# Result stores moved between DMA queues and transfers spaced differently in an attention plus MLP-mixer kernel

## The chip, the cores and the metric

The kernel runs on one core of one Trainium2 chip. The metric is device time in microseconds (us) from start to end of one execution; the median of several runs is given.

The core's engines are named as the profile names them: PE (TensorE, matrix products; PEld is its weight load), DVE (VectorE), ACT (ScalarE), POOL (GpSimd) and SP (SyncE, which only issues transfers here). Each works through its own instruction list in order. SP and ACT also issue DMAs ("SPq" and "ACTq" in the profile); an instruction that waits holds up everything behind it in its engine's list.

## The reference

Attention with normalized queries and keys over 8 batches, 12 heads, 448 positions and head size 64, and then a mixer MLP on the result, all in float32:

```python
q_n, k_n = rmsnorm(q, g_q), rmsnorm(k, g_k)
attn = softmax(q_n @ k_n.T / sqrt(64))
x = (attn @ v), heads side by side          # per batch: 448 x 768
h = relu(x.T @ w_tok1) @ w_tok2             # token mixing: 448 -> 256 -> 448
u = x + h.T
out = u + relu(u @ w_ch1) @ w_ch2           # channel mixing: 768 -> 1536 -> 768
```

## The kernel before, in words

The work goes batch by batch. Attention handles two pairs of heads at a time in four steps; while the mixer of batch b runs, the attention of batch b+1 is interleaved with it. What each engine does, and in which order, is written out by hand: the code builds lists of items, each a function with a cost in microseconds; `merge` interleaves lists so that each advances in proportion to its share of cost, and `run` calls the items in order and adds their costs to a model clock. A function given to `later(us, fn)` is called when that clock has advanced by `us`. The costs serve the interleaving alone.

The activations stand transposed: `uT` holds 768 channels (6 blocks of 128) by 448 positions. For one batch the mixer goes through these stages:

- **x.** The token mixing needs x with positions on the partitions. For batches after the first, DVE transposes 32x32 blocks of `uT` into `xt` (L615), four DMAs write it to memory (`send_x`, L585, tile `xs`, runs of 128 bytes), and one DMA reads it back (`load_x`, L590, 672 KB). This is done in two halves of three blocks, both in the last part of the batch before.
- **Token mixing.** `tok1` (L629, relu by ACT at L632), then six products `tok2` (L637), each added into `uT` by DVE (L642); `moving_sums` (L658 to L661) prepares sums for the next stage. Products use two PSUM banks in turn (`m_ps`), so a product waits until DVE or ACT has emptied the bank of the product two before it.
- **Channel products.** Batches after the first use a seven-product scheme on 2x2 blocks: `ch1` (L761), `ch2` with two column blocks (L818), and last `ch2` with one column block, seven items of 2.24 us that `last_items` lists. The weights come from memory in units of 384 KB (L687); six buffers, and the load of a unit is issued five units ahead.
- **Result.** DVE transposes each of the six blocks of `uT` into a tile `turned` (`trans_y`, L855, four buffers), and four DMAs each (`send_y`, L577, 56 KB, runs of 128 bytes) write it to the output. For all batches but the last, all six are done inside the token mixing of the next batch, and ACT issues their DMAs.

In batch 0 the weights are also split into blocks and stored (L193), and sums of weight blocks are formed by POOL (load L203, sums L206 to L209, store L211); most of these sums fall into batch 1.

Queries and keys are loaded by SP (L1071, for most pairs eight DMAs of 56 KB), each followed by a squares pass on ACT (L1090), row sums on DVE (L1104), a fold on ACT (L1112), a chain of small DVE operations for the inverse root (L1121 to L1147), scaling (L299) and two transposes (L314). Values come by L287. The row sums of the exponentials (L376) are formed by POOL and DVE.

Every DMA of the compiled program signals its landing on one of eight semaphores, given out in turn over both queues, and waits first for the DMA that used its semaphore before.

Of the kernel before, what the change touches and what calls it, by code (L numbers as in the profile page):

```python
# [8 lines left out]
F32 = mybir.dt.float32  # L9
# [35 lines left out]
def whole(ctx, tc, shifted, pre, q, k, v, g_q, g_k, moe_w_tok1, moe_w_tok2, moe_w_ch1, moe_w_ch2, out):  # L45


    nc = tc.nc
# [7 lines left out]
    P = 128  # L56
# [58 lines left out]

    def later(us, fn):

        pending.append((clock[0] + us, fn))

    def run(items):  # L120
        for c, fn in items:
# [341 lines left out]
    def att_step(g):  # L463


        t, s = divmod(g, 4)
        p = 2 * t
        pair = (p, p + 1)
        live = g < NG
        items = []  # L470

        def finish():
            if s == 0 and t:
                last = (p - 2, p - 1)
                for k in (NK - 2, NK - 1):
                    values(last, k)
            if live:
                for k in ((0,), (1, 2), (3, 4), (5, 6))[s]:
                    score(t, k)
            if s == 0 and t:  # L480
                if not on_pe(p - 1):
                    row_sums(t - 1)
                for i in last:
                    st.pop(("v", i))

        def tiled():
            if shifted:
                if live:
                    both_shifted()
            else:  # L490
                finish()
            if live and s == 3:
                for i in pair:
                    st.pop(("qkT", i))
            if inside:
                for fn in turns:
                    fn()
            if live and s and not shifted:
                for k in ((), (0,), (1, 2), (3, 4))[s]:
                    values(pair, k)  # L500

        def both_shifted():
            i = p + s // 2
            if s % 2 == 0:
                score_shifted(i)
                return
            for k in range(NK):
                values((i,), k)
            for k in range((NK + 1) // 2):
                st.pop(("e1", i, k))  # L510
            st.pop(("v", i))
            for part in denominators((i,)):
                part()

        n = p + 2
        ahead, behind, turns = [], [], []
        f = lambda fn, *pairs: [lambda i=i: fn(i, st) for i in pairs]
        scales = lambda n: [lambda i=i: scale(i) for i in (n, n + 1)]  # L520
        if g in (1, 5):
            ahead, behind = f(pre.square, g // 4 * 2 + 4), f(pre.reduce, g // 4 * 2 + 4)
        elif g in (2, 6):
            ahead, behind = f(pre.square, g // 4 * 2 + 5), f(pre.reduce, g // 4 * 2 + 5)
        elif g in (3, 7):
            behind = pre.roots(g // 4 * 2 + 4, st)
        elif g in (4, 8):
            behind = scales(g // 4 * 2 + 2)
        if live and n < NP:
            late = n < 2 * NPAIR + 2  # L530
            if t >= NPAIR // 2 and late:
                if s == 1:
                    ahead, behind = f(pre.square, n), f(pre.reduce, n) + f(pre.square, n + 1)
                elif s == 2:
                    behind = f(pre.reduce, n + 1) + pre.roots(n, st) + scales(n)
            elif t >= NPAIR // 2:
                a, b = f(pre.square, n) + f(pre.reduce, n), f(pre.square, n + 1) + f(pre.reduce, n + 1)
                behind = (a, b + pre.roots(n, st), scales(n), [])[s]
            now = {2: [] if pre.plain(n) else [n], 3: [n, n + 1] if pre.plain(n) else [n + 1]}.get(s, [])
            turns = [lambda q=q, i=i: turn_qk(q, i) for q in now for i in (1, 0)]  # L540

        inside = g < 2 * NPAIR
        items += [(0.3, fn) for fn in ahead]
        items.append((2.4 if s == 1 else 3.2, tiled))
        part = lambda fns, c=0.4: [(c, fn) for fn in fns]
        if s == 0 and t and not shifted:
            items += part(denominators((p - 2, p - 1)))
        if live and not on_pe(p):
            items += [(0.5, lambda k=k: group_sums(t, k)) for k in ((), (1, 2), (3, 4), (5, 6))[s]]

        if s == 0 and 5 < p + 1 < NP:
            items.append((0.0, lambda: load_v(p + 1)))
        if live and s == 1 and 5 < p + 2 < NP:
            items.append((0.0, lambda: load_v(p + 2)))
        js = []
        if live and s == 0:
            js = [n, n + 1] if pre.plain(p) else [n + 1]
        elif live and s == 3 and not pre.plain(n):
            js = [n + 2]
        items += [it for j in js if pre.first_slot + 2 <= j < NP  # L560
                  for it in part(pre.loads(j, st, nc.sync, nc.sync), 0.2)]
        if g == 3:
            items += [it for j in (6, 7) for it in part(pre.loads(j, st, nc.sync, nc.sync), 0.2)]
        items += part(behind)
        if not inside:
            items += part(turns)
        return items
# [4 lines left out]


    def send_y(b, cc, t):
        dst = out[b][:, cc * P:(cc + 1) * P]
        for i in range(0, P, 32):
            nc.scalar.dma_start(  # L577
                out=dst[:, i:i + 32].rearrange("(n t) c -> t n c", t=32),
                in_=t[i:i + 32].rearrange("t (n c) -> t n c", c=32))

    def send_x(b, half, t):

        xs = st["xs"] = xs_pool.tile([KC * S, P], F32, name="xs")
        for i in range(0, P, 32):
            nc.sync.dma_start(  # L585
                out=xs[:, i:i + 32].rearrange("(n t) c -> t n c", t=32),
                in_=t[i:i + 32].rearrange("t (n c) -> t n c", c=32))

    def load_x(b, half):
        nc.sync.dma_start(  # L590
# [7 lines left out]
    def trans_x(b, j):  # L598

        half, o = divmod(j, KC)  # L600
        if b == 0:

            if o == 0:
                x_tile(b, half)
            ps = s_tile("t_ps")
            for c in range(NS):
                nc.tensor.transpose(
                    ps[0:R, c * P:(c + 1) * P], st["uT", b][:, j, c * R:(c + 1) * R], ident[:, :])
            nc.scalar.copy(  # L609
                out=st["x", b, half][0:R, o], in_=ps[0:R, :].rearrange("p (c n) -> p c n", c=NS))  # L610
            return

        if j == 0:
            st["xt"] = tu_pool.tile([P, 2, KC, S], F32, name="xt", tag="tu")
        nc.vector.transpose(out=st["xt"][:, half, o, :], in_=st["uT", b][:, j, :])  # L615
        if o == KC - 1:
            t = st["xt"][:, half].rearrange("p j s -> p (j s)")
            if half:
                st.pop("xt")
            later(2.0, lambda: send_x(b, half, t))  # L620
            later(6.0, lambda: load_x(b, half))

    def tok1(b, jc, h):
        cs = slice(h * HC, (h + 1) * HC)
# [225 lines left out]
            into(nc.vector, 1, 0, got)  # L850

    def trans_y(b, cc):

        t = turn_pool.tile([P, S], F32, name="turned")
        nc.vector.transpose(out=t[:], in_=st["uT", b][:, cc, :])  # L855
        later(2.0, lambda: send_y(b, cc, t))

    def turns(b, cs):
        return [(0.3, lambda cc=cc: trans_y(b, cc)) for cc in cs]

    us = lambda n, cols: n * cols * 4 / 2400

# [21 lines left out]
    def in_next(b):  # L884


        return b < B - 1 and not shifted

    def last_items(b, sums):

        single = [(us(6, HS), lambda i=i: ch2(b, 1, i, 0)) for i in range(7)]
        if b == 0:
            single = merge(
                [(us(6, S), lambda o=o, h=h: ch2_first(o, h, 2)) for o in range(2) for h in range(2)], sums)
        l = [] if in_next(b) else turns(b, [0, 1, KC, KC + 1])
        return [single[0]] + merge(single[1:-1], l) + [single[-1]]


# [51 lines left out]
    for b in range(B):  # L950
        early, double = middle_items(b)
        if b == 0:
            begin = x_items(0, 1) + tok1_items(0, 0) + tok1_items(0, 1)
            early = merge(begin + early, weight_items(BEFORE, then)) + merge(
                double, weight_items(then, len(chunks) + 3) + sums[:6])
        else:

            run(merge(tok1_items(b, 0), left[:2]))
            begin, early = merge(tok1_items(b, 1) + early[:3 * KC], left[2:]), early[3 * KC:]
            if b == 1:  # L960
                early, double = merge(begin + early, sums[12:33]), merge(double, sums[33:])
                begin = []
            early = begin + early + double
# [6 lines left out]
        if b + 1 < B:  # L970
            last = merge(last, x_items(b + 1, 1))
        run(merge(att, early) + last + last_items(b, sums[6:12]))
        left = turns(b, range(NC) if in_next(b) else [2, KC + 2])
    run(left)
    for _, fn in pending:
        fn()
# [245 lines left out]
```

## Time and profile before

| | us |
|---|---|
| median of 9 runs | 1367.56 |
| lowest, highest | 1363.66, 1375.27 |
| the profiled execution's own time | 1365.98 |
| its span (first to last instruction) | 1364.2 |
| PE busy | 1289.1 |
| DVE busy | 749.8 |
| POOL, ACT busy | 369.0, 367.0 |

The token mixing of batches 0 to 7 begins at about 99, 273, 447, 605, 764, 922, 1078 and 1237 us of the span; the stretch between two of these is one period, some 156 to 160 us in the later batches. The profile gives busy times of engines, what ended each idle time ("<-DMA unit<-ws" is the landing of a transfer into a tile `unit`), and for DMAs the time from issue to landing. A number like L637 is a line of the kernel.

### The profile page before, as it was taken

The page shows a single profiled execution, that of the slowest core. Times are in us where ns is not written, and L with a number is a line of the kernel's source. Part 1 is how long each engine was busy: PE and PEld are TensorE (multiplying, and loading weights), DVE is VectorE, ACT ScalarE, POOL GpSimd, SP SyncE. Part 2 cuts the span into 40 slices and gives each one's busy share as a digit, 9 for nine tenths or more (in the row PEclk, how much of TensorE's full clock was granted, in tenths as well). Part 3 has the DMA queues.
Part 4 walks back from the last instruction along what each step waited for, and adds up shares of the span by engine and source line. Part 5 has one row for each costly group of instructions (what it writes and reads, how often), then busy time and mean ns, then how long its engine had stood idle before and what let it go on. Part 6 is the DMA issues. An engine that isn't in the chain of part 4 may idle for free.

```text
span 1364.2 us, 20203 instructions
## 1 busy us (share of the span) xinstructions
PE 1289.1 (94%) x7408; PEld 925.0 (68%) x7408; DVE 749.8 (55%) x1295; ACT 367.0 (27%) x734; POOL 369.0 (27%) x406
## 2 busy tenths in 40 slices
PE   4889999979998999999999999999999989999996
PEld 2344444437687588785878667785878758787996
DVE  6988987236673556616663275635566165343212
ACT  5553442023220243203331133302332123200100
POOL 1202111347562233103331132312241124211220
PEclk9899999989999999999999999999999989999998
DMA  9695877988899566694559765694667845385654
GB/s 197 184 248 166 236 199 207 252 218 216 232 245 227 129 162 161 152 228 93 153 129 207 167 130 139 160 239 78 161 165 163 215 82 159 105 197 137 180 172 113
DMA packets 508144, 238.83 MB, mean 175 GB/s; under 512 B 374084, under 2 KB 466628, under 8 KB 508036
## 3 DMA queue, kind: packets, MB, share of 16 engines
q1 hardware_dynamic: 416962, 225.97, 65.2%
q10 hardware_dynamic: 90946, 11.48, 5.3%
q8 instruction: 61, 1.00, 0.3%
q14 instruction: 47, 0.39, 0.1%
q0 software_dynamic: 128, 0.00, 0.0%
HBM read 197.85 MB, written 39.52 MB: 174 GB/s over the span
## 4 chain that ended last, share of the span: by engine, by line
PE 74%; DVE 9%; DMA 7%; SPq 3%; ACT 2%; issue 2%; ACTq 1%; POOL 1%; DVEq 0%
PE m_ps L761 24%; PE m_ps L818 19%; PE s_ps L334 7%; PE o_ps L408 7%; PE m_ps L629 6%; DMA unit<-ws 4%; PE m_ps L742 4%; PE m_ps L724 4%; PE m_ps L637 2%; SPq L1071 1%; ACTq L577 1%; PE d_ps L388 1%; DVE es L376 1%; DVE uT L642 1%; DVE qk_t L299 1%
## 5 line engine op out<-in xcount | busy, mean ns | idle before, releaser
L818 PE MATMUL m_ps<-hb,unit 128*128 128x224 f32 x1764 | 343.9, 354 | 14.3 <-DMA unit<-ws 13.8
L818 PEld LDWEIGHTS m_ps<-hb,unit 128*128 128x128 f32 x1764 | 330.5, 190 | 33.4 <-issue 22.9
L761 PE MATMUL m_ps<-tu,unit 128*128 128x224 f32 x1008 | 203.3, 357 | 2.7 <-DVE hb L766 2.4
L761 PEld LDWEIGHTS m_ps<-tu,unit 128*128 128x128 f32 x1008 | 190.2, 191 | 19.0 <-issue 5.6
L338 ACT ACTIVATE e<-s_ps 128x448 f32<-128x448 f32 x336 | 157.2, 547 | 132.2 <-PE s_ps L334 97.7
L761 PE MATMUL m_ps<-uT,unit 128*128 128x224 f32 x756 | 152.3, 355 | 0.3 <-DVE uT L642 0.3
L761 PEld LDWEIGHTS m_ps<-uT,unit 128*128 128x128 f32 x756 | 141.4, 190 | 14.8 <-DVE qkT L314 6.3
L334 PE MATMUL s_ps<-qkT 64*64 64x448 f32 x1260 | 148.4, 558 | 2.0 <-ACT x L609 1.9
L408 PE MATMUL o_ps<-e,v 64*64 64x448 f32 x1316 | 149.3, 540 | 0.1
L827 POOL TENSOR_TENSOR uT<-uT,r 128x448 f32<-128x448 f32 (+1 forms) x56 | 50.6, 913 | 278.8 <-DVE r L827 146.8
L766 DVE TENSOR_TENSOR r<-m_ps,r 128x448 f32<-128x448 f32 x63 | 39.3, 623 | 132.5 <-PE m_ps L761 94.0
L827 DVE TENSOR_TENSOR uT<-uT,m_ps 128x448 f32<-128x448 f32 (+1 forms) x70 | 33.8, 500 | 140.9 <-PE m_ps L818 140.9
L376 DVE TENSOR_TENSOR es<-es,e 128x896 f32<-128x896 f32 x84 | 97.0, 1155 | 10.2 <-ACT e L338 7.3
L637 PE MATMUL m_ps<-w_sb,h 128*128 128x448 f32 x192 | 82.9, 573 | 17.3 <-DVE uT L642 14.8
L408 PEld LDWEIGHTS o_ps<-e,v 64*64 64x64 f32 x1316 | 49.9, 133 | 68.6 <-issue 62.4
L1104 DVE TENSOR_REDUCE ms<-sq 128x28 f32<-128x896 f32 (+2 forms) x47 | 51.3, 1091 | 81.3 <-ACT sq L1090 78.8
L376 POOL TENSOR_TENSOR es<-e 128x896 f32<-128x896 f32 x21 | 44.4, 2112 | 186.6 <-ACT e L338 186.6
L334 PEld LDWEIGHTS s_ps<-qkT 64*64 64x64 f32 x1260 | 44.1, 135 | 73.9 <-issue 60.8
L629 PE MATMUL m_ps<-x,w_sb 112*128 112x384 f32 x256 | 86.0, 489 | 0.0
L766 POOL TENSOR_TENSOR hb<-r,r 128x448 f32<-128x448 f32 x21 | 23.8, 1134 | 226.5 <-ACT r L782 226.5
L637 PEld LDWEIGHTS m_ps<-w_sb,h 128*128 128x128 f32 x192 | 35.8, 195 | 61.1 <-DVE uT L642 29.7
L317 ACT ACTIVATE qkT<-qkT,g_t 128x448 f32<-128x448 f32 x36 | 24.0, 668 | 195.2 <-DVE qkT L314 183.7
(100 smaller groups left out, 1358.6 us busy)
## 6 DMA issues: line engine op xcount, KB each, us to landing
unit<-ws SPq DMA_DIRECT2D x318, 384.0 KB, 4.0
raw<-in_moe_w_ch_dram SPq DMA_DIRECT2D x72, 256.0 KB, 3.7
out_dram<-turned ACTq DMA_DIRECT2D x192, 56.0 KB, 2.0
v<-in_v_dram SPq DMA_DIRECT2D x94, 112.0 KB, 5.0
xs<-xt SPq DMA_DIRECT2D x56, 168.0 KB, 4.4
x<-xs SPq DMA_DIRECT2D x14, 672.0 KB, 7.2
ws<-stage SPq DMA_DIRECT2D x36, 256.0 KB, 3.8
raw<-ws SPq DMA_DIRECT2D x36, 256.0 KB, 4.6
```

The costliest lines, as they stand in the source:

```text
L334: nc.tensor.matmul(out=pss[i][rows_of(i, a), 0:S], lhsT=qkT[h, 1, k * D:(k + 1) * D], rhs=qkT[h, 0, :], start=True, stop=True)
L338: nc.scalar.activation(out=e[:, i, :], in_=pss[i][:, 0:S], func=AF.Exp)
L376: eng.tensor_tensor(out=es[:], in0=(es if k > 1 else st["e", t, 0])[:], in1=st["e", t, k][:], op=ALU.add)
L408: nc.tensor.matmul(out=st["o", p][a * D:(a + 1) * D, 0:S], lhsT=vt[rows, k * D:(k + 1) * D], rhs=e[rows, :], **kw)
L629: nc.tensor.matmul(out=ps[:, 0:HC], lhsT=w1_sb[0:R, c, jc * P:(jc + 1) * P], rhs=st["x", b, h][0:R, :, c, :], start=(c == 0), stop=(c == N ...
L637: nc.tensor.matmul(out=ps[:, 0:S], lhsT=st["h1", jc][:, cc * P:(cc + 1) * P], rhs=w2_sb[:, jc].rearrange("p c r -> p (c r)"), start=(jc == ...
L724: nc.tensor.matmul(out=ps[:, 0:S], lhsT=st["w"][t // KC][:, t % KC, j, :], rhs=u[:, t, :], start=(t == 0), stop=(t == 2 * KC - 1))
L742: nc.tensor.matmul(out=ps[:, 0:S], lhsT=w, rhs=natural(half)[:, :, t, :], start=(half == 0 and t == 0), stop=(half == 1 and t == KF - 1))
L761: nc.tensor.matmul(out=ps[:, j * HS:(j + 1) * HS], lhsT=w[:, t, j, :], rhs=m, start=(t == 0), stop=(t == KC - 1))
L766: add = lambda e, o, x, y: e.tensor_tensor(out=o, in0=x, in1=y, op=ALU.add)
L818: nc.tensor.matmul(out=ps[:, j * HS:(j + 1) * HS], lhsT=st["w"](j, t), rhs=hb[:, HB[what], t, :], start=(t == 0), stop=(t == KF - 1))
L827: add = lambda e, o, x, y: e.tensor_tensor(out=o, in0=x, in1=y, op=ALU.add)
```

## The change

- `send_y` issues through SP for every batch but the last.
- Four of the six turns of a batch (blocks 0, 1, 3 and 4) are done among the seven last channel products of the batch itself; their DMAs are issued in the next batch's token mixing (`sends`). Blocks 2 and 5 are still turned and sent there.
- `send_x` issues its four DMAs at steps of 2 on the model clock and not at once; `load_x` follows 12 after the turn and not 6. `later` keeps its list sorted by due time.
- The items that load queries and keys count 0.6 each and not 0.2, for the pairs that use eight DMAs.

```diff
@@ -115,7 +115,11 @@
 
     def later(us, fn):
 
-        pending.append((clock[0] + us, fn))
+        at = clock[0] + us
+        i = len(pending)
+        while i and pending[i - 1][0] > at:
+            i -= 1
+        pending.insert(i, (at, fn))
 
     def run(items):
         for c, fn in items:
@@ -558,7 +562,7 @@
         elif live and s == 3 and not pre.plain(n):
             js = [n + 2]
         items += [it for j in js if pre.first_slot + 2 <= j < NP
-                  for it in part(pre.loads(j, st, nc.sync, nc.sync), 0.2)]
+                  for it in part(pre.loads(j, st, nc.sync, nc.sync), 0.2 if pre.plain(j) else 0.6)]
         if g == 3:
             items += [it for j in (6, 7) for it in part(pre.loads(j, st, nc.sync, nc.sync), 0.2)]
         items += part(behind)
@@ -572,19 +576,24 @@
 
 
     def send_y(b, cc, t):
+
         dst = out[b][:, cc * P:(cc + 1) * P]
         for i in range(0, P, 32):
-            nc.scalar.dma_start(
+            (nc.sync if in_next(b) else nc.scalar).dma_start(
                 out=dst[:, i:i + 32].rearrange("(n t) c -> t n c", t=32),
                 in_=t[i:i + 32].rearrange("t (n c) -> t n c", c=32))
 
     def send_x(b, half, t):
 
+
         xs = st["xs"] = xs_pool.tile([KC * S, P], F32, name="xs")
-        for i in range(0, P, 32):
+
+        def part(i):
             nc.sync.dma_start(
                 out=xs[:, i:i + 32].rearrange("(n t) c -> t n c", t=32),
                 in_=t[i:i + 32].rearrange("t (n c) -> t n c", c=32))
+        for i in range(0, P, 32):
+            later(i / 16, lambda i=i: part(i))
 
     def load_x(b, half):
         nc.sync.dma_start(
@@ -618,7 +627,7 @@
             if half:
                 st.pop("xt")
             later(2.0, lambda: send_x(b, half, t))
-            later(6.0, lambda: load_x(b, half))
+            later(12.0, lambda: load_x(b, half))
 
     def tok1(b, jc, h):
         cs = slice(h * HC, (h + 1) * HC)
@@ -850,13 +859,19 @@
             into(nc.vector, 1, 0, got)
 
     def trans_y(b, cc):
-
-        t = turn_pool.tile([P, S], F32, name="turned")
+        t = st["y", cc] = turn_pool.tile([P, S], F32, name="turned")
         nc.vector.transpose(out=t[:], in_=st["uT", b][:, cc, :])
-        later(2.0, lambda: send_y(b, cc, t))
-
-    def turns(b, cs):
-        return [(0.3, lambda cc=cc: trans_y(b, cc)) for cc in cs]
+
+    def turns(b, cs, send=True):
+
+        def one(cc):
+            trans_y(b, cc)
+            if send:
+                later(2.0, lambda: send_y(b, cc, st.pop(("y", cc))))
+        return [(0.3, lambda cc=cc: one(cc)) for cc in cs]
+
+    def sends(b, cs):
+        return [(0.3, lambda cc=cc: send_y(b, cc, st.pop(("y", cc)))) for cc in cs]
 
     us = lambda n, cols: n * cols * 4 / 2400
 
@@ -892,7 +907,7 @@
         if b == 0:
             single = merge(
                 [(us(6, S), lambda o=o, h=h: ch2_first(o, h, 2)) for o in range(2) for h in range(2)], sums)
-        l = [] if in_next(b) else turns(b, [0, 1, KC, KC + 1])
+        l = turns(b, [0, 1, KC, KC + 1], not in_next(b))
         return [single[0]] + merge(single[1:-1], l) + [single[-1]]
 
 
@@ -955,6 +970,9 @@
                 double, weight_items(then, len(chunks) + 3) + sums[:6])
         else:
 
+            if in_next(b - 1):
+                y, z = sends(b - 1, [0, 1, KC, KC + 1]), left
+                left = [y[0], y[1], z[0], y[2], z[1], y[3]]
             run(merge(tok1_items(b, 0), left[:2]))
             begin, early = merge(tok1_items(b, 1) + early[:3 * KC], left[2:]), early[3 * KC:]
             if b == 1:
@@ -970,7 +988,7 @@
         if b + 1 < B:
             last = merge(last, x_items(b + 1, 1))
         run(merge(att, early) + last + last_items(b, sums[6:12]))
-        left = turns(b, range(NC) if in_next(b) else [2, KC + 2])
+        left = turns(b, [2, KC + 2])
     run(left)
     for _, fn in pending:
         fn()
```

## The prediction

> **What bounds the kernel now.** I read the page first, then the waits, then the timelines of the two kinds of place where TensorE stops.
>
> ```profile
> PE 1289.1 (94%) x7408; PEld 925.0 (68%) x7408; DVE 749.8 (55%) x1295; ACT 367.0 (27%) x734; POOL 369.0 (27%) x406
> PEclk9899999989999999999999999999999989999998
> out_dram<-turned ACTq DMA_DIRECT2D x192, 56.0 KB, 2.0
> ```
>
> TensorE (PE) is busy 1289.1 of 1364.2 us at nearly the full clock, so all that any change of order can win lies in 75.1 us of idle time. The table of busy time by stretch splits that: 30.0 us lie before 130 us (loading, first attention) and 11.5 us after 1237.7 (mostly the last results leaving); the change touches neither much. About 34 us are left, of which batch 1's period (273 to 450) holds 13.7. The waits say what ended the sizeable ones:
>
> ```profile
> PE m_ps L637 <- DVE uT L642: 14.8, 10, 4.5
> PE m_ps L818 <- DMA unit<-ws: 13.8, 14, 2.1
> PE m_ps L637 <- ACT h L632: 2.5, 1, 2.5
> ```
>
> (Columns: total us, times, longest.) One kind is late weight units in the last channel products of a batch (L818), the other a late update of uT in the token mixing that opens the next batch (L637). The timelines of PE, SP and ACT show each:
>
> ```profile
> 903.65 9.32 PE L818 MATMUL m_ps<-hb,unit 128*128 128x224 f32 x48 [0.52 <-DMA unit<-ws]
> 920.26 2.51 PE L818 MATMUL m_ps<-hb,unit 128*128 128x224 f32 x12 [2.07 <-DMA unit<-ws]
> ...
> 289.91 2.29 PE L637 MATMUL m_ps<-w_sb,h 128*128 128x448 f32 x4 [2.50 <-ACT h L632]
> 300.94 1.59 PE L637 MATMUL m_ps<-w_sb,h 128*128 128x448 f32 x2 [4.46 <-DVE uT L642]
> ```
>
> ```profile
> 902.05 6.91 SPq L585 DMA_DIRECT2D xs<-xt  x4
> 909.06 1.41 SPq L687 DMA_DIRECT2D unit<-ws  x2
> 911.59 0.32 SPq L590 DMA_DIRECT2D x<-xs  x1
> 912.00 4.26 SPq L687 DMA_DIRECT2D unit<-ws  x5
> ```
>
> ```profile
> 280.80 6.71 ACTq L577 DMA_DIRECT2D out_dram<-turned  x4
> 287.62 1.85 ACT L338 ACTIVATE e<-s_ps 128x448 f32<-128x448 f32 x4 [6.38 <-DMA out_dram<-turned]
> ```
>
> At 912 us five units stand behind 672 KB of x; the first took 8.1 us to land and PE stood still. At 280.8 us ACT spent 6.71 us issuing four result DMAs; the exponentials and the relu behind them in its queue were late, then the squares, VectorE's (DVE's) norm chain, and the uT updates behind that chain.
>
> [...] one result DMA costs ACT 492 ns in the median, one query DMA of equal size costs SP 477. [...] 374084 of 508144 packets are under 512 B, and the DMA engines are 98% busy at 227 GB/s while queries and keys pass (890 to 900) but 107% at 326 GB/s once units dominate (915 to 920).
>
> **The change part by part.** The program's order before and after, engine by engine, shows the same 10437 PE and 5613 DVE instructions; 168 DMAs go from ACT's list (1905 to 1737) to SP's (2002 to 2170).
>
> *Result DMAs to SP, 24 in each of seven batches.* ACT loses 24 x 0.49 = 11.8 us of issue per batch, all in the token mixing. SP gains as much; there it is idle (no issue from 605.4 to 633.8), so that costs nothing; without that cover each would delay the units by 0.5 us. The compiled waits add a second effect: every DMA takes one of eight landing semaphores and waits for the DMA eight places earlier, whichever queue holds it. ACT therefore waited for SP's landings (the 6.71 us) and SP for DMAs that ACT had not issued yet: the store of weight sums at 280.05 left as the result DMA of 278.22 landed. On one queue that crossing is gone.
> - Head of batch 1: 2.50 + 4.46 + 0.45 = 7.4 us stood still. ACT no longer stops, so the norm chain starts some 5 us earlier. SP is full here with weight sums, and eight result DMAs stand behind three of them; I leave 2.0 us of stall. Gain 5.4 (0 to 7.4).
> - Head of batch 6 (gap of 3.25 at 1094.23): same cause, with squares at 1093.3 behind result DMAs. Afterwards PE does four products more behind the attention step, and the chain starts about 3 us earlier; I leave 0.5. Gain 2.7.
>
> *Four of six turns (0.63 us each on DVE) into the last products.* A product takes 2.24 us of PE and its eviction 0.39 of DVE, two PSUM buffers deep: 0.39 + 0.63 is covered, cost nothing (0.6 a batch if the cover fails). The fifth turn stays at the head of the token mixing and needs a buffer (four in all) that the first result DMAs free: see the second rival.
>
> *Heads of batches 2 to 5.* Here the order gets slightly worse. PE: 16 matmul records of L629 (5.2 us), attention (2.4), 16 more (5.2), one product L637 (1.6), attention (3.2), three products (4.8), attention (3.2), two products. DVE does the second uT update when its product ends at 19.3 us, and then 1.1 (row sum) + 1.1 (moving sums) + 0.6 (turn) + 1.1 (row sum) + 2.1 (scaling) before the third, which ends near 26.6, where PE wants its bank at 25.7. With the row sums ahead of the sixth update I count 1.7 us of stall against 0.96 before. Loss 0.75 x 4 = 3.0 (0 to 8).
>
> *x in steps, its load at 12 instead of 6, queries and keys at 0.6.* In the order after, x's four stores alternate with units, and three units that stood behind x stand ahead of it; of each group of query and key DMAs four or five go behind two units. Stalls of units behind x: 0.97 + 1.37 + 2.07 + 0.63 = 5.0, taken as gone. The other 8.8 (behind queries, keys or x's stores) I halve: 4.4. Bytes before the next batch are the same and the DMA engines are full from 890 to 925, so I charge back 2.5. Gain 6.9 (0 to 11). x's second half may now come later: issue some 6 us before the token mixing, 7.2 to landing (median), first use 7.6 us into it: 6 us of cover.
>
> *Attention merged at another pace with the channel products.* The trace can't show it; PE has no stall in those stretches. Bounds: 1 us gained (0.62 at 213.5 us) to 6 lost; I take 2.0 lost.
>
> Sum: 5.4 + 2.7 - 3.0 + 6.9 - 2.0 = 10.0 us. Against the profiled execution's 1365.98: 1356.0. The median of the runs stands 1.6 above that: **1357.5**.
>
> **The rivals.**
> *The DMA window only shifts.* Speaks for it: over 100% busy with the same bytes. Then the tails give nothing: 10.0 - 6.9 = 3.1, so 1364.5. Against: stalls hang on which bytes come first.
> *Slower: DVE waits for the result's buffers.* In DVE's order the fifth turn stands ahead of the squares' row sum, which is wanted about 10 us into the token mixing. Its buffer comes free when four result DMAs have landed[...]. I expect 6 to 8 us, as the backlog before was gone by 928 us, 5.4 into the mixing. If they land at 15 us, each head loses 4 to 5 us: 6 x 4.5 = 27, less the 10, gives 1384; it decides from about 11 us on, and breaks even near 12.
> *x arrives late.* If its landing grows to 17 us, PE waits 3 us in each of six heads: 1375. Against: the 6 us of cover.
> That the change does nothing is excluded by the order.
>
> **How the numbers follow.** About 0.3% (4 us) is what a measurement of this kernel can tell from no change. Forecast 0.57 (own range 1349 to 1363), nearly all faster; shifted window 0.22, half within 0.3%; buffers 0.14, of which a mild case ends near 1369; x late 0.07. Faster 0.68, same 0.13, slower 0.19. The range 1349 to 1370 takes in the bounds of the parts and the mild ends of the rivals.
>
> **What would show it.** Right: no result DMA on ACT but the last batch's; L818 waiting for units about half of 13.8 us; heads of batches 1 and 6 with gaps under 2 us; heads of 2 to 5 with about 1.7. Wrong: DVE idle before the fifth turn until a result DMA lands; L629 waiting for x; new waits of PE in the middle of a batch; unit waits as large as before.

## The result, and the profile after

The changed kernel takes 1359.64 us in the median of 10 runs (1357.73 to 1361.84), against 1367.56 in the median of 31 runs of the kernel before that lie beside it: ratio 0.9936, 95% interval 0.9918 to 0.9955. The profiled execution took 1356.59 us (before 1365.98), its span is 1354.8 us.

The page of the kernel after, the lines that answer to those shown of before (busy time; granted clock in 40 slices; the result's DMAs):

```profile
PE 1287.9 (95%) x7408; PEld 925.1 (68%) x7408; DVE 753.4 (56%) x1295; ACT 365.1 (27%) x734; POOL 368.2 (27%) x406
PEclk9899999999998999999999999999999999999999
out_dram<-turned SPq DMA_DIRECT2D x168, 56.0 KB, 2.0
```

PE's idle time fell from 75.1 to 66.9 us, and 168 result DMAs are on SP's queue, with the same 2.0 us from issue to landing. What PE waited for, kernel after (total us, times, longest):

```profile
PE m_ps L646 <- DVE uT L651: 7.0, 6, 2.0
PE m_ps L827 <- DMA unit<-ws: 6.6, 4, 5.1
PE m_ps L770 <- DVE r L775: 4.1, 9, 0.8
PE m_ps L751 <- DMA unit<-ws: 3.6, 1, 3.6
PE m_ps L770 <- ACT r L791: 3.1, 5, 0.6
```

The lines of before have moved: L637 is now L646, L818 is L827, L761 is L770. Updates of uT that came late cost 7.0 us instead of 14.8, units of the last products (L827) 6.6 instead of 13.8. Other waits have grown: the channel products L770 wait 7.2 us for the sums `r` of their own scheme to be taken out of PSUM (0.3 before), and one unit in batch 0 comes 3.6 us late (L751; 0.6 before, there L742).

By period (from the start of one token mixing to the next, us), one profiled execution each:

| batch | 0 | 1 | 2 | 3 | 4 | 5 | 6 | 7 |
|---|---|---|---|---|---|---|---|---|
| before | 173.7 | 174.4 | 157.6 | 159.7 | 158.1 | 155.5 | 159.4 | 126.7 |
| after | 176.6 | 167.7 | 158.5 | 158.7 | 158.7 | 157.8 | 152.8 | 125.1 |

The gain is in batches 1, 6 and 7 (14.9 us); batches 0 and 2 to 5 together lost 5.7. At the head of batch 1, the timeline of ACT, then of PE, kernel after:

```profile
284.28 1.85 ACT L342 ACTIVATE e<-s_ps 128x448 f32<-128x448 f32 x4 [0.42 <-PE s_ps L338]
285.99 0.97 ACT L1108 ACTIVATE sq<-qk_t 128x896 f32<-128x896 f32 x1
```

```profile
304.00 1.77 PE L646 MATMUL m_ps<-w_sb,h 128*128 128x448 f32 x4 [1.22 <-DVE uT L651]
```

ACT starts the exponentials 0.42 us after it fell idle, where it had waited 6.38 us behind its own result DMAs, and PE's stop of 4.46 us is one of 1.22. The head of batch 6 runs without a stop (PE, before, then after):

```profile
1097.48 3.36 PE L637 MATMUL m_ps<-w_sb,h 128*128 128x448 f32 x4 [3.25 <-DVE uT L642]
1100.77 3.01 PE L334 MATMUL s_ps<-qkT 64*64 64x448 f32 x16
```

```profile
1096.12 6.55 PE L646 MATMUL m_ps<-w_sb,h 128*128 128x448 f32 x16
```

But the end of batch 1 got worse. Timelines of PE and of SP's queue, kernel after:

```profile
403.22 7.08 PE L827 MATMUL m_ps<-hb,unit 128*128 128x224 f32 x36
415.40 2.95 PE L827 MATMUL m_ps<-hb,unit 128*128 128x224 f32 x7 [5.10 <-DMA unit<-ws]
```

```profile
403.43 1.95 SPq L1089 DMA_DIRECT2D qk_t<-in_q_dram  x2
405.42 3.38 SPq L1089 DMA_DIRECT2D qk_t<-in_k_dram  x3
...
409.98 0.44 SPq L696 DMA_DIRECT2D unit<-ws  x1
```

The unit was issued at 409.98 us, behind five DMAs of queries and keys and two of the weight sums; PE stood still from 410.30 (403.22 + 7.08).

### The profile page after: what moved, and what is told of

The parts are those of the page before. It is cut to its first block, busy times and chain, and to the rows that moved or that the text cites. A ratio compares the mean times of both kernels' runs of the same rounds, so it can differ in the third digit from the quotient of the medians.

```text
span 1354.8 us, 20152 instructions
## 1 busy us (share of the span) xinstructions
PE 1287.9 (95%) x7408; PEld 925.1 (68%) x7408; DVE 753.4 (56%) x1295; ACT 365.1 (27%) x734; POOL 368.2 (27%) x406
## 4 chain that ended last, share of the span: by engine, by line
PE 74%; DVE 12%; DMA 5%; SPq 3%; ACT 2%; issue 2%; POOL 2%; DVEq 0%; ACTq 0%; POOLq 0%
PE m_ps L827 22%; PE m_ps L770 19%; PE s_ps L338 7%; PE o_ps L412 7%; PE m_ps L638 6%; PE m_ps L733 4%; PE m_ps L751 4%; DMA unit<-ws 3%; PE m_ps L646 3%; DVE qk_t L303 2%; DVE es L380 2%; PE d_ps L392 1%; DVE qkT L318 1%; ACT e L342 1%; DVE uT L651 1%
## 5 line engine op out<-in xcount | busy, mean ns | idle before, releaser
L827 PE MATMUL m_ps<-hb,unit 128*128 128x224 f32 x1764 | 343.9, 356 | 6.7 <-DMA unit<-ws 6.6
L827 PEld LDWEIGHTS m_ps<-hb,unit 128*128 128x128 f32 x1764 | 333.4, 191 | 23.6 <-issue 16.8
L770 PE MATMUL m_ps<-tu,unit 128*128 128x224 f32 x1008 | 202.8, 356 | 4.4 <-DVE r L775 3.0
L770 PEld LDWEIGHTS m_ps<-tu,unit 128*128 128x128 f32 x1008 | 188.3, 190 | 23.4 <-DVE r L775 5.5
L770 PE MATMUL m_ps<-uT,unit 128*128 128x224 f32 x756 | 155.0, 357 | 6.4 <-ACT r L791 3.1
L770 PEld LDWEIGHTS m_ps<-uT,unit 128*128 128x128 f32 x756 | 140.5, 190 | 23.2 <-DVE uT L651 7.0
L380 DVE TENSOR_TENSOR es<-es,e 128x896 f32<-128x896 f32 x84 | 94.2, 1122 | 13.2 <-ACT e L342 10.0
L775 POOL TENSOR_TENSOR hb<-r,r 128x448 f32<-128x448 f32 x21 | 27.8, 1326 | 227.6 <-ACT r L791 174.9
L380 POOL TENSOR_TENSOR es<-e 128x896 f32<-128x896 f32 x21 | 44.7, 2127 | 161.7 <-ACT e L342 161.7
L646 PE MATMUL m_ps<-w_sb,h 128*128 128x448 f32 x192 | 79.5, 557 | 7.1 <-DVE uT L651 7.0
L638 PE MATMUL m_ps<-x,w_sb 112*128 112x384 f32 x256 | 86.0, 489 | 0.0
L638 PEld LDWEIGHTS m_ps<-x,w_sb 112*128 112x128 f32 x256 | 47.9, 190 | 35.7 <-ACT e L342 4.9
```

Source lines behind the costliest of these rows:

```text
L380: eng.tensor_tensor(out=es[:], in0=(es if k > 1 else st["e", t, 0])[:], in1=st["e", t, k][:], op=ALU.add)
L638: nc.tensor.matmul(out=ps[:, 0:HC], lhsT=w1_sb[0:R, c, jc * P:(jc + 1) * P], rhs=st["x", b, h][0:R, :, c, :], start=(c == 0), stop=(c == N ...
L646: nc.tensor.matmul(out=ps[:, 0:S], lhsT=st["h1", jc][:, cc * P:(cc + 1) * P], rhs=w2_sb[:, jc].rearrange("p c r -> p (c r)"), start=(jc == ...
L770: nc.tensor.matmul(out=ps[:, j * HS:(j + 1) * HS], lhsT=w[:, t, j, :], rhs=m, start=(t == 0), stop=(t == KC - 1))
L775: add = lambda e, o, x, y: e.tensor_tensor(out=o, in0=x, in1=y, op=ALU.add)
L827: nc.tensor.matmul(out=ps[:, j * HS:(j + 1) * HS], lhsT=st["w"](j, t), rhs=hb[:, HB[what], t, :], start=(t == 0), stop=(t == KF - 1))
```

## The experiments

Each kernel was timed in five rounds beside the kernel before on the same chip. Its median there was 1366.98 us beside e1 to e4, 1366.36 beside e6 to e9, 1365.69 beside e5, e10 and e12, and 1365.95 beside e11; beside the kernel after it was 1367.56. So a difference of medians between two kernels of different groups is good to some 2 us. Where that matters, the difference of their ratios to before, times 1367 us, is given as well.

| kernel | result's queue | turns | x in steps | pace 0.6 | median us | ratio to before, 95% |
|---|---|---|---|---|---|---|
| before | ACT | old | no | no | 1365.7 to 1367.6 | 1 |
| e2 | SP | old | no | no | 1350.67 | 0.9879 (0.9851 to 0.9907) |
| e6 | ACT | old | yes | no | 1354.86 | 0.9908 (0.9877 to 0.9939) |
| e7 | ACT | old | no | yes | 1379.97 | 1.0101 (1.0065 to 1.0137) |
| e9 | SP | old | yes | no | 1334.71 | 0.9769 (0.9734 to 0.9803) |
| e1 | SP | new | yes | no | 1335.34 | 0.9775 (0.975 to 0.98) |
| e3 | SP | new | no | yes | 1364.24 | 0.9983 (0.9963 to 1.0003) |
| e4 | SP | old | yes | yes | 1360.63 | 0.9951 (0.9932 to 0.997) |
| e5 | ACT | new | yes | yes | 1367.88 | 1.0015 (1.0002 to 1.0029) |
| after | SP | new | yes | yes | 1359.64 | 0.9936 (0.9918 to 0.9955) |

**e1: the pace undone.**

```diff
-  for it in part(pre.loads(j, st, nc.sync, nc.sync), 0.2 if pre.plain(j) else 0.6)]
+  for it in part(pre.loads(j, st, nc.sync, nc.sync), 0.2)]
```

> The changed kernel with the items that load queries and keys counted 0.2 again and not 0.6; all else as changed. Theory A (the wider pace costs more than it brings): batches 2 to 5 lose 3.0 us each of small TensorE stalls in the first channel products (about 3.7 to 0.8 a period) and 0.9 us each for one more border between attention and mixer, and batch 0 its 3 us stall for units; the waits of the last channel products for units come back in part, up to 1.1 us a period. 1359.6 - 15.6 - 2.9 + 4.4 = 1345 to 1350 us. Theory B (the pace is what freed the units): unit waits of the last products return to some 10 us in batches 2 to 5 and the first channel products keep their stalls: 1366 to 1370 us.

Measured 1335.34 us: the direction of A at about twice the size (A had 10 to 15 us). The pace costs 24.3 us beside the other edits (22.0 by the ratios). What PE waited for in e1, the rows that answer to the ones above:

```profile
PE m_ps L646 <- DVE uT L651: 7.4, 9, 1.8
PE m_ps L827 <- DMA unit<-ws: 2.7, 2, 1.8
PE m_ps L751 <- DMA unit<-ws: 1.5, 1, 1.5
```

The rows of L770 waiting for `r` are gone, and so are most waits for units, though the DMAs of queries and keys leave closer together here. Periods 2 to 5 take 153.5 to 153.9 us, and 158.5 to 158.7 (157.8 in batch 5) in after: 18.8 us in the four; batch 1 takes 161.7 for 167.7. These two are the cost in these two profiles, with 2.1 given back in batch 6.

**e2: the queue alone** (the kernel before with this edit).

```diff
-  nc.scalar.dma_start(
+  (nc.sync if in_next(b) else nc.scalar).dma_start(
```

> The kernel before with one edit: the result's DMAs go from SP's queue, all six turns of a batch still in the next batch's token mixing. Theory A (crossing of the two queues was what stopped ACT and the weight sums): the gaps at the heads of batches 1 and 6 (7.4 and 3.25 us of idle, and the half clock after them) shrink to under 2 us each, unit waits stay as before (about 13 us): 1367.6 - 10 to 13 = 1355 to 1358 us. Theory B (DVE waits for the four buffers of turned blocks whichever queue empties them): the gaps stay, within 2 us of the kernel before.

Measured 1350.67 us, 16.3 less than before: more than either theory gave. One queue edit alone is worth twice what the whole change brought. PE's waits in e2:

```profile
PE m_ps L818 <- DMA unit<-ws: 13.0, 14, 1.9
PE m_ps L637 <- DVE uT L642: 7.7, 9, 1.8
```

This is what A expected to see: the stops in the token mixing shrink from 17.3 us (14.8 and 2.5) to 7.7, the unit waits stay (13.8 before). These 9.6 us fall short of the 16.3; the clock can account for up to 5 of the rest (last section).

**e3: x at once again.**

```diff
-  later(i / 16, lambda i=i: part(i))
+  part(i)
...
-  later(12.0, lambda: load_x(b, half))
+  later(6.0, lambda: load_x(b, half))
```

> The changed kernel with x's four stores issued at once again and its load at 6 and not 12 on the model clock. Theory A (x's order against the units is what freed the last products): waits for units in the last channel products go from 1.5 us in batches 2 to 5 to 5 to 8 us; 1364 to 1367 us. Theory B (the spread of queries and keys did it): under 2 us more; 1359 to 1361 us.

Measured 1364.24 us: A, 4.6 us more than after (6.4 by the ratios). In batches 2 to 5 PE waits 6.8 us for units, 1.5 in after.

**e4: all six turns in the next batch's token mixing again** (`last_items` without turns, `sends` left out).

```diff
-  left = turns(b, [2, KC + 2])
+  left = turns(b, range(NC) if in_next(b) else [2, KC + 2])
```

> The changed kernel with all six turns in the next batch's token mixing again, sent from SP there. Theory A (the four turns are covered where they are now and in the way where they were): each head has 0.6 to 1 us more, 1363 to 1365 us. Theory B (the turns do not matter once ACT does not issue): within 2 us of the changed kernel, 1358 to 1361. Theory C (the turns' place is what shifts DVE's order into the stalls of the first channel products): these stalls fall by 3 us a period, 1350 us.

Measured 1360.63 us: B. It is 1.0 us above after (2.1 by the ratios), and the intervals of the two ratios overlap, so no worth of the turns can be told from nothing here.

**e7: the pace alone** (the kernel before with the first line of e1's diff).

> The kernel before with one edit: a DMA of queries or keys counts 0.6 us in the merged order in place of 0.2. Theory A (the wider pace costs time by itself: on TensorE's order it spreads the attention further through the token mixing, whose products with x then wait more often for VectorE's r and ScalarE's r): the 24 us that e1 gave back come out here too, 1385 to 1393. Theory B (the pace costs only beside the result's DMAs on SP's queue, which take turns with the DMAs of queries and keys): within 4 us of before, 1363 to 1371.

Measured 1379.97 us, 13.6 more than before: between the two theories. The pace costs by itself, whatever queue the result is on. That it costs less here than beside the other edits has one reason in the traces: here it also spares waits for units, 5.2 us in batches 2 to 5 for 10.3 before, and beside the other edits there are none left to spare (0.1 in e1). The rest of the difference isn't placed.

**e6: x in steps alone** (the kernel before with e3's diff reversed, and the sorted `later`).

> The kernel before with the DMAs of x alone spread: the four stores at steps of 2 us, the load back 12 us after the turn in place of 6. Theory A (the weights of the channel products that follow on the same queue land earlier, whatever else is on it): the 4.6 us that e3 lost come as a gain, 1361 to 1364. Theory B (the gain needs the result's DMAs to be on SP's queue, where they and x meet): within 2 us of before, 1365 to 1369.

Measured 1354.86 us, 11.5 less than before, over twice A's gain. What PE waited for in e6 (its L825 and L749 are after's L827 and L751):

```profile
PE m_ps L825 <- DMA unit<-ws: 4.0, 3, 2.2
PE m_ps L749 <- DMA unit<-ws: 2.2, 1, 2.2
```

Batches 2 to 5 hold 0.5 us of this, 10.3 before. So spreading x settles the units of the later batches by itself; it needs neither the queue nor the pace.

**e9: queue and x in steps** (turns and pace undone).

> The kernel after, with the pace undone as in e1 and all six turns in the next batch's token mixing as in e4: so the kernel before with the result's DMAs on SP's queue and x in steps. Theory A (the turns' place is worth nothing, as e4 said): within 3 us of e1, 1333 to 1339. Theory B (the turns' place pays once the pace no longer covers it, by the 0.6 us a batch and the first mixing's head that they free): 1340 to 1347. The sum of e2's gain and of the 5 us of x in steps alone would give 1346.

Measured 1334.71 us: A. Queue and x together give 31.6 us, 3.8 more than the sum of each alone (16.3 and 11.5). The period of batch 3 as one stretch (us, then busy time of PE, PEld, DVE, ACT and POOL, granted clock, DMA share, GB/s), first kernel after, then e9:

```profile
601.70:760.40 158.70, 155.35 (x921) 117.12 (x920) 85.61 (x152) 41.70 (x87) 40.01 (x32) 1.00 0.67 157
```

```profile
588.60:742.50 153.90, 153.35 (x922) 117.45 (x921) 85.44 (x152) 42.02 (x87) 40.76 (x32) 1.00 0.68 162
```

The same work at the same clock: e9 leaves PE idle for 0.55 us of this period, after for 3.35, and the rest of the difference sits in PE's "busy" column, whose ends of matmuls are modelled.

**e5: the result on ACT's queue again.**

> The kernel after, with the result's DMAs on ACT's queue again; turns, x and pace stay. Theory A (the queue is worth the same 16 us with or without the other edits): 1374 to 1379. Theory B (a kernel whose period is set by the wider pace has less of it to gain, since the turns and x already relieve the same heads): 1360 to 1368.

Measured 1367.88 us: B, at the upper edge of its range. The queue is worth 8.2 us beside the pace (10.8 by the ratios), 20.1 without it (e6 to e9). This kernel, pace, x and turns together, is no faster than before: the pace had eaten all that x in steps brings.

**e8: the sum of the pace without its steps.**

```diff
-  ... 0.2 if pre.plain(j) else 0.6)]
+  ... 0.2)
+  + ([] if pre.plain(j) else part([lambda: None] * 8, 0.4))]
```

> The kernel after, with the DMAs of queries and keys at 0.2 us each again, but behind each group of eight of them stand eight empty items of 0.4 us that issue nothing: the sum of the merged order is that of after, the DMAs themselves leave at the earlier pace. Theory A (what costs is the sum, which spreads the attention's products over more of the token mixing): as after, 1356 to 1362. Theory B (what costs is where the DMAs of queries and keys stand on SP's queue, ahead of weights and x): as e1, 1334 to 1341. In between, both have a share.

Measured 1374.87 us (ratio 1.0049, 1.0026 to 1.0071), outside both. PE's waits in e8 (its L828, L771, L752 are after's L827, L770, L751):

```profile
PE m_ps L828 <- DMA unit<-ws: 17.2, 10, 4.7
PE m_ps L771 <- DVE r L776: 6.5, 12, 0.8
PE m_ps L752 <- DMA unit<-ws: 6.5, 1, 6.5
```

With the attention spread as in after, bunched DMAs of queries and keys do make the units late: 23.7 us of waits, 10.2 in after. So the wide steps do what a reader of the diff would think they do: they free the units. But they mend only a part of what their own weight in the merged list breaks: e8 is 39.5 us above e1, and the steps bring back 15.2 of it.

**e10: the same length, laid evenly.** This is e1, and the attention's step functions count 1.6 us more each, in the first attention too.

```diff
-  items.append((2.4 if s == 1 else 3.2, tiled))
+  items.append((4.0 if s == 1 else 4.8, tiled))
```

> The kernel after, with the DMAs of queries and keys at 0.2 us each again and the difference, 6.4 us for each group of four attention steps, laid evenly on the four steps (2.4 and 3.2 us become 4.0 and 4.8). The attention's list is as long as after's and the clock that releases the results and x advances as there. Theory A (the unevenness costs: wide loads in two of four steps leave long unbroken runs of channel products, which the evictions on DVE and ACT can't follow, and attention steps close together elsewhere): as e1, 1333 to 1340. Theory B (the length of the list or the faster clock costs): as after or e8, 1358 to 1375.

Measured 1351.22 us (0.9896, 0.9869 to 0.9924): between. The waits for `r` and the stops at the heads of batches 2 to 5 are gone, so these two come from the uneven spread. Waits for units are back instead, 7.1 us in batches 2 to 5. Of the 15.9 us above e1, 3.4 lie before the first token mixing, where after has no edit. So a longer list costs something even when it is laid evenly.

**e11: uneven, but no longer.** e1 with

```diff
+  u = (1.6, -1.6, -1.6, 1.6)[s] if live and t >= 5 else 0
+  items.append(((2.4 if s == 1 else 3.2) + u, tiled))
```

> The kernel of e1 (DMAs of queries and keys at 0.2) with the attention's step functions themselves weighted unevenly from the pairs of batch 1 on: the first and fourth of each four count 1.6 us more, the second and third 1.6 less. The list is as long as e1's, the clock and the number of DMAs are the same; the spread is nearly that of after. Theory A (what the wide pace costs is its unevenness): the runs of 48 products come back, and with them VectorE's and ScalarE's r late for the next product: 1345 to 1360. Theory B (the length of the list, the clock or the place of the DMAs costs, as the rest of e10 suggests): 1333 to 1339.

Measured 1358.98 us (0.994, 0.9914 to 0.9966): A by its number, but not by its reason. Waits of PE in e11 (its L828 and L647 are after's L827 and L646):

```profile
PE m_ps L828 <- DMA unit<-ws: 12.3, 6, 7.4
PE m_ps L647 <- DVE uT L652: 10.0, 12, 2.1
```

There is no wait of a channel product for `r`; the loss is in late units and in uT, and it lies elsewhere: 12.3 us over e1 in batch 1 and 9.3 in batches 2 to 5, where after loses 6.0 and 18.8. Shown is that an uneven spread is enough to cost 24 us with nothing else changed. Not shown is that it always costs through `r`, nor that e11's spread is the one of after.

**e12: 0.05 for a DMA of queries and keys** (after with 0.05 in place of 0.6).

> The kernel after, with a DMA of queries and keys at 0.05 us in the merged order, so below the 0.2 of before. Theory A (the less the loads weigh, the more even the products lie between attention steps): 1328 to 1335, under e1. Theory B (0.2 is near a best point: below it the DMAs bunch on SP's queue and the units behind them come late): 1338 to 1350.

Measured 1334.84 us (0.977, 0.9735 to 0.9804): inside A's range, but level with e1 and e9, so nothing is left in that direction. e1, e9 and e12 are the fastest kernels here, 2.3% under before and 1.8% under after (1334.7 / 1359.6); they can't be told apart.

**Where the pace costs inside a period.** Timelines of PE and DVE in batch 3, kernel after:

```profile
640.58 7.08 PE L770 MATMUL m_ps<-tu,unit 128*128 128x224 f32 x36
648.28 2.54 PE L770 MATMUL m_ps<-uT,unit 128*128 128x224 f32 x12 [0.62 <-ACT r L791]
```

```profile
643.15 0.62 DVE L775 TENSOR_TENSOR r<-m_ps,r 128x448 f32<-128x448 f32 x1 [4.98 <-PE m_ps L770]
643.70 0.64 DVE L441 STREAM_TRANSPOSE dt<-d_ps 128x448 f32<-128x448 f32 x1
...
647.14 0.62 DVE L458 TENSOR_TENSOR uT<-o_ps,rd 128x448 f32<-128x448 f32 x1
647.68 0.61 DVE L775 TENSOR_TENSOR r<-m_ps,r 128x448 f32<-128x448 f32 x1
```

and the same stretch in e1:

```profile
636.04 2.43 PE L770 MATMUL m_ps<-uT,unit 128*128 128x224 f32 x12
638.41 1.73 PE L338 MATMUL s_ps<-qkT 64*64 64x448 f32 x16
```

```profile
637.96 0.62 DVE L458 TENSOR_TENSOR uT<-o_ps,rd 128x448 f32<-128x448 f32 x1
639.12 0.62 DVE L775 TENSOR_TENSOR r<-m_ps,r 128x448 f32<-128x448 f32 x1 [0.54 <-POOL r L775]
```

DVE scales an attention result in eight instructions, 4.0 us (643.70 to 647.68). In after, four products (12 matmuls each) stand in a row on PE over this time. The second ends near 645.3, but DVE takes it up only at 647.68 and holds its bank until 648.29. The fourth product starts at 648.28, before that and 0.05 us after ACT's copy has emptied the bank of the third (648.22). So the row names the right one: the fourth took the third's bank, and the two banks are not taken strictly in turn here. The second's bank would have let it start no earlier. PE stops 0.62 us because neither bank was free before. That DVE's eight instructions are what kept the second's bank is read from the order of its list; no run moves them alone. In e1 an attention step stands on PE where the fourth product stood, and the same eight instructions cost nothing.

A row of 48 matmuls takes 9.35 us where nothing stops it. Before and e1 have two such rows in this period, both at 9.35; after has three, and they take 10.24, 9.80 and 10.38. In the third the same eight instructions of DVE stand beside the row (687.32 to 691.31), in the second a sum of DVE waits for POOL. That is 2.4 us of the 5.2 that this period lost to e1 (158.7 and 153.5). The rest is smaller: 0.6 in an attention step whose `d_ps` products were cut up (640.58 stands after 3.76 us of attention in place of 3.17), 0.5 at the head (0.96 against 0.44), 0.3 where the second channel product waits for uT, 0.4 in units, and some 1.0 that I can't place.

## Why the prediction was right, and where its sum was not

The time, 1357.5 us predicted and 1359.64 measured, was right; the sum of parts behind it was not. It set the heads, the queue and the units at 12.0 us gained (5.4 + 2.7 - 3.0 + 6.9; the 6.9 counts in what the pace does for the units), and the pace's effect on the attention at 2.0 lost. The runs show 31.6 us gained without the pace (before to e1) and 24.3 lost by it (22.0 by the ratios). The two sides were off in opposite directions by about 20 us each, so the close total is luck.

- **Head of batch 1, 5.4 us.** Right in mechanism and size: of 7.4 us of stops 1.6 are left (2.0 predicted), a gain of 5.8. The whole period gained 6.7: at its end the unit wait grew from 3.48 to 5.10 us, while a wait for `hb` among its channel products shrank from 2.41 to 1.31 and the clock was at half for 6.8 us and not for 10.2.
- **Head of batch 6, 2.7 us.** Right: 3.25 us of stop are gone. The period gained 6.6; most of the surplus is a term that the prediction didn't have, the clock (below): the two rows of before that follow the stop took 3.36 and 3.01 us, rows of their size take 1.77 and 1.73 elsewhere, so 2.9 us.
- **The queue as a whole.** 8.1 us predicted for these two heads; 8.2 measured beside the pace (e5; 10.8 by the ratios), 16.3 alone, 20.1 with x in steps. The prediction took the two large stops for all that the queue costs, and had no clock. Between e6 and e9, one profile each, the period of batch 1 shrinks by 13.1 us, batch 6 by 3.2, batches 2 to 5 by 3.4 together. Batch 0, which sends no result, shrinks by 4.1 as well; the mean granted clock of these two profiled executions was 0.985 (e6) and 0.995 (e9). How much of the rest is the crossing of landing semaphores and how much ACT's 0.49 us per issue, no run separates.
- **Turns at nothing.** Not contradicted: without the new turns the time is 1.0 us higher in e4 than in after (2.1 by the ratios) and 0.6 lower in e9 than in e1, neither clear of noise.
- **Heads of batches 2 to 5, 3.0 us lost.** Too large: the stop at the third update is 0.96 us (0.9 by the prediction's own 26.6 and 25.7), but the sixth update adds only 0.34, where it had counted the rest of 1.7. That is 1.30 against 0.96 before, 1.4 us lost in the four batches. And it goes with the pace: in e1 each head stops for 0.43 or 0.44.
- **x in steps and pace on the units, 6.9 us.** The residue was predicted at about half of 13.8 and L827 shows 6.6, but in other places: batches 2 to 5 keep 1.5 of 10.3 us, batch 1 has 5.10 and batch 0 has 3.6 (L751) that were 3.48 and 0.6. The steps of x alone give 11.5 us (e6), so the charge of 2.5 us for full DMA engines and the halving of 8.8 us were both too cautious, and for batches 2 to 5 the queries' and keys' wide steps weren't needed.
- **Attention at another pace, 2.0 us lost, at most 6.** This is the step that failed most. The reason was "PE has no stall in those stretches". That a stretch has no stall says only that the order of before fits; it doesn't bound what another order costs. The place of attention steps among channel products decides whether DVE's 4.0 us of scaling falls beside attention or beside a row of products. It could be counted beforehand from two known lists: rows of 48 matmuls without an attention step between them go from two in a period to three, and DVE's scaling falls beside two of them.

Rivals: that DVE waits for the result's buffers at the fifth turn was not decisive. In batches 2 to 6 its buffer came free, and the turn began, 3.5 to 4.8 us into the token mixing, sooner than the 6 to 8 predicted. In batch 1 it waited longer, until 10.9 us, but the squares' row sum behind it was not held up. Timeline of DVE, kernel after:

```profile
286.37 0.65 DVE L863 STREAM_TRANSPOSE turned<-uT 128x448 f32<-128x448 f32 x1 [10.11 <-DMA out_dram<-turned]
287.00 1.08 DVE L1122 TENSOR_REDUCE ms<-sq 128x28 f32<-128x896 f32 x1
```

The squares themselves end at 286.96 on ACT, so the row sum could not have started before. The shifted DMA window is refuted for batches 2 to 5 by e6, and x late shows in no wait of the products that read it (L638).

## What to carry to other kernels

When several edits come together, one of them can cost more than the rest bring; undo each by itself, and do it first for the edit that seems only to change the order on the busiest engine. A weight in an interleaving list is not only a spacing of the items that carry it: it moves everything else in that list, and the order on the bound engine must be counted with the evictions that run beside it. In the kernel before, the DMAs of two issuing queues shared eight landing semaphores, and each queue waited for the other: ACT took 6.71 us for four issues at 280.80 us, and SP waited 113.4 us in all (74.1 at L1071, 30.7 at L687, 8.6 at L211) for result DMAs to land, three rows that the kernel after doesn't have. Putting them on the queue of the engine that computes nothing took that away, and the issue time on ACT (0.49 us each) with it, and was worth 16.3 us here (e2).

## What was not expected of the hardware

In the traces of before and after, PE's granted clock falls to half for 3.4 or 6.8 us after a short stop. Stretches of the kernel after (columns as in the stretches of after and e9 above: length, busy time of PE, and so on; the clock is the third number from the end):

```profile
124.00:127.40 3.40, 1.40 (x4) 0.49 (x3) 3.33 (x7) 0.72 (x1) 0.00 (x0) 1.00 0.00 0
127.40:130.80 3.40, 3.40 (x9) 1.73 (x8) 3.30 (x6) 0.53 (x1) 0.00 (x0) 0.50 0.78 231
...
209.30:212.70 3.40, 1.65 (x5) 0.55 (x3) 3.24 (x5) 1.72 (x3) 0.00 (x0) 1.00 1.04 316
...
410.70:414.10 3.40, 0.00 (x0) 0.00 (x0) 0.86 (x2) 0.00 (x0) 1.63 (x3) 1.00 1.02 280
414.10:420.90 6.80, 5.50 (x15) 5.03 (x16) 1.09 (x1) 0.95 (x1) 0.00 (x0) 0.50 1.10 274
```

After a stretch with 1.40 us of work the clock is at half. But a stop of 3.56 us (210.95 to 214.51) left it at full speed, longer as it is than the 2.00 us that fall into the first row: it lies across two stretches, and each still holds work (1.65 us in the one shown, 1.59 us in the next). The changes of the clock lie on one grid of 3.41 us: 127.38 and 414.10 are 84 steps apart, and in before 301.26, 349.05 and 1096.56 us are 3, 17 and 236 steps behind 291.02. So the stop of 2.00 us cost more than its length and the longer one of 3.56 us did not, by where they fell.

How much work the steps of this grid held can be read from the traces of before and after together (99 to 1320 us, PE's busy time as the profile models it). At full clock, each of the 6 steps in which PE was busy for 0.41 of the time or less was followed by half the clock; none of the other 700, which held 0.47 or more, was. At half clock, the two steps with 0.62 and 0.73 were followed by half again, and the six in which PE was busy all the time by full clock. So the stop of 5.10 us cost two steps: the first one at half clock held 0.62.

Behind the first token mixing (99 us) and ahead of the end, half the clock was granted for 17.1 us in the profile of before and 10.2 in that of after. The mean granted clock of these two profiled executions was 0.987 and 0.990, of e9's 0.995. But this varies between executions of one kernel (0.984 to 0.992 for before). The mean clock over all runs on record is 0.9882 for before (those beside the experiments), 0.9887 for after, 0.9915 for e2 and 0.9933 for e9. An estimate from these: the time lost to the lower clock is at most the missing share of the span, 16.1, 15.4, 11.5 and 8.9 us. So the clock explains about 1 us of what the change brought, up to 5 of the 16.3 us of e2 and up to 7 of the 31.6 us of e9.
